# Batch 0's linear term from (h w1) w_out, its hwd in four pieces, and pooling sums two units at a time

## The chip, the cores and the metric

The kernel runs on one core of one Trainium2 chip. The metric is device time in microseconds (us). A core has five engines with instruction queues of their own: TensorE (PE in the profile, with its weight loads as PEld), VectorE (DVE), ScalarE (ACT), GpSimd (POOL) and SyncE (SP), and 16 DMA engines. TensorE writes its results to PSUM, which has 8 banks of 128 partitions by 512 fp32 values; VectorE and ScalarE carry them on to SBUF.

## What is computed

```python
# x (4, 12544, 128), inducing (32, 128); w1, w2 (128, 1024); w_out (1024, 128)
def mab(q, kv):
    s = scale * (q @ kv.transpose(0, 2, 1))     # scale = 1 / sqrt(128)
    s = s - s.max(-1, keepdims=True)
    a = np.exp(s)
    a /= a.sum(-1, keepdims=True) + 1e-09
    return a @ kv
h = mab(I, x)              # I: inducing for each of the 4 batches; h is (4, 32, 128)
y = mab(x, h)              # (4, 12544, 128)
t = y.reshape(50176, 128)
out = np.maximum(t @ w1, t @ w2) @ w_out        # (50176, 128)
```

The kernel never builds y. With e the exponentials of a token over the 32 rows of h, and d their sum, t = (e h) / d, and

out = (e (h w1) w_out + relu(e h(w2 - w1)) w_out) / d.

The first term is the linear term: `m1` = (h w1) w_out is 32 x 128 for each batch. `hwd` is h(w2 - w1), 32 x 1024 for each batch. A chunk is 128 tokens; there are 98 chunks in each of 4 batches, 8 final matmuls (one for each 128 of the 1024 hidden values) for each chunk, 3136 in all.

## The kernel before

Everything is recorded in the order in which a small clock in the kernel believes it best. Batch 0 has a first part of its own (transposes, scores, sums). Then the main loop goes through the finals of all batches and puts between them the phases, the stages of exponentials and the pooling of the next batch. The queues of the engines hold what was recorded, in that order.

The handover from batch 0's sums to the loop:

```python
nc.vector.tensor_scalar(out=w1h, in0=w1h, scalar1=-1.0, ...)
sums = small_h(0)          # hT4: h transposed, four copies side by side; es: the sums of exponentials
weights_2()                # transposes of w1h -> w1T
small_sums(*sums)          # rs, rw: reciprocals of the sums, with scales
stage(blocks[0])
small_hwd(0, (0,))
blocks[0].staged = max(blocks[0].staged, st[0]["hwdr"])
small_hwd(0, (1,))
stage(blocks[1])
# ...
phase(plan_phase(False))
weights_3()                # w1out = w1 w_out
phase(plan_phase(False))
pending.append((small_m1, (0,)))
```

```python
def small_hwd(b, halves=(0, 1)):
    # ...
    for half in halves:
        for n in range(2 if b == 0 and half == 0 else 1):
            w = 256 if b == 0 and half == 0 else 512
            # ...
            if b == 0:
                nc.tensor.matmul(out=ps, lhsT=hT4, rhs=w2h[:, sl], start=True, stop=False)
                nc.tensor.matmul(out=ps, lhsT=hT4, rhs=w1h[:, sl], start=False, stop=True)
            else:
                nc.tensor.matmul(out=ps, lhsT=hT4, rhs=w21[:, sl], start=True, stop=True)
            # half 0, n 0: VectorE to hwd (times rw for batch 0); the others: ScalarE
            # ...

def small_m1(b):           # m1 = h w1out
    nc.tensor.matmul(out=ps[:, 0:128], lhsT=hT4, rhs=w1out, start=True, stop=True)
    # ... VectorE to m1bd and m1

def weights_2():           # 2 banks of 4 transposes: one copied by VectorE, one by ScalarE
    # ...
def weights_3():           # 8 matmuls w1T x woutp in one bank, then ScalarE to w1out
    # ...
```

(`hT4`, `ps` stand for the entries of `st[b]` and the bank taken.) One unit of pooling, 16 chunks of the next batch; a batch has six units and two chunks over:

```python
def pool_accum(b, u):
    bi, ps = bank([128, 512])
    # ...
    for j in range(4):
        for g in range(4):
            nc.tensor.matmul(out=ps[32 * g : 32 * (g + 1), 0:128],
                             lhsT=eT[:, j, 32 * g : 32 * (g + 1)],
                             rhs=xn_of(b, U * u + 4 * g + j),
                             start=(j == 0), ..., tile_position=(0, 32 * g))
    # ... last unit: the two chunks over, and their sums
    if u == 0:
        nc.vector.tensor_copy(out=hacc, in_=ps[:, 0:128])
    else:
        nc.vector.tensor_add(out=hacc, in0=ps[:, 0:128], in1=hacc)
```

In the loop, a phase (`phase`, line 957) is up to four row-packed jobs, one for each quarter of 32 partitions, each of 512 columns into a bank of its own: e times hwd for relu, or e times m1 for the linear term. Each bank of relu is evicted by ScalarE (line 973) or VectorE (line 976). A final (`final_one`, line 792) is one 128x128 matmul of relu by woutp. A group of up to 4 chunks, 32 finals, is evicted by VectorE (line 819, times the reciprocal of d) and stored. `stage` (line 582, line 594) makes the exponentials of a block; `dens` (line 622) their sums. `keep_busy` (line 749) puts in matmuls of zeros where the kernel's clock expects TensorE to wait:

```python
for _ in range(n):
    nc.tensor.matmul(out=g.ps[:, 0:256], lhsT=warm[:, 0:128], rhs=warm[:, 0:256],
                     start=False, stop=False, skip_group_check=True)
```

Three forms of TensorE's array alternate: the whole array (finals, sums, transposes), packed by rows (phases), packed by columns (stage, pooling).

The relu buffers have two slots for each quarter; w2h and w1h are loaded into a slot of quarters 0 and 1:

```python
w2h = relup.tile([128, 4096], F16, name="w2h", tag="relu0")[:, 0:J]
w1h = relup.tile([128, 4096], F16, name="w1h", tag="relu1")[:, 0:J]
```

Of the kernel before, what the change touches and what calls it, by code (L numbers as in the profile page):

```python
# [9 lines left out]
F16 = mybir.dt.float16  # L10
F32 = mybir.dt.float32
AF = mybir.ActivationFunctionType
# [90 lines left out]
def kernel(  # L103
# [93 lines left out]
    with tc.manual_schedule(engines={ET.PE, ET.DVE, ET.Activation, ET.Pool, ET.SP}):  # L197
# [150 lines left out]

        def pool_accum(b, u):
            bi, ps = bank([128, 512])  # L350
            ck.wait(ck.bank[bi], "p1")
            eT = st[b]["eT", u][0]
            st[b]["sum", u] = True
            last = u == NU - 1
            for j in range(4):
                for g in range(4):
                    nc.tensor.matmul(  # L357
                        out=ps[32 * g : 32 * (g + 1), 0:128],
                        lhsT=eT[:, j, 32 * g : 32 * (g + 1)],
                        rhs=xn_of(b, U * u + 4 * g + j),  # L360
                        start=(j == 0),
                        stop=(j == 3 and not (last and g < REST)),
                        tile_position=(0, 32 * g),
                        skip_group_check=True,
                    )
            if last:
                et = st[b]["et"][0]
                for g in range(REST):
                    for rhs, lo, n in ((xn_of(b, U * NU + g), 0, 128), (ones16[:, 0:1], 128, 1)):
# [8 lines left out]
                        )  # L378
            end = ck.run(0.26, "col")
            if u == 0:  # L380
                st[b]["hacc"] = smp.tile([128, C], F32, name=f"hacc_{b}", tag="hacc")
                nc.vector.tensor_copy(out=st[b]["hacc"], in_=ps[:, 0:128])
            else:
                acc = st[b]["hacc"]
                nc.vector.tensor_add(out=acc, in0=ps[:, 0:128], in1=acc)
# [61 lines left out]

        def small_hwd(b, halves=(0, 1)):
            if 0 in halves:
                st[b]["hwd"] = smp.tile([128, J], F16, name=f"hwd_{b}", tag="hwd")  # L450
            hwd = st[b]["hwd"]
            for half in halves:
                for n in range(2 if b == 0 and half == 0 else 1):
                    w = 256 if b == 0 and half == 0 else 512
                    bi, ps = bank([128, 512])
                    ps = ps[:, 0:w]
                    sl = slice(512 * half + w * n, 512 * half + w * (n + 1))
                    ck.wait(max(ck.bank[bi], st[b]["hT4r"]), "p1")
                    if b == 0:
                        nc.tensor.matmul(out=ps, lhsT=st[b]["hT4"], rhs=w2h[:, sl], start=True, stop=False)  # L460
                        nc.tensor.matmul(out=ps, lhsT=st[b]["hT4"], rhs=w1h[:, sl], start=False, stop=True)
                        end = ck.run(0.43 * w / 512)
                    else:
                        nc.tensor.matmul(out=ps, lhsT=st[b]["hT4"], rhs=w21[:, sl], start=True, stop=True)  # L464
                        end = ck.run(0.215)
                    if half == 0 and n == 0:
                        if b == 0:
                            nc.vector.tensor_scalar(
                                out=hwd[:, sl], in0=ps, scalar1=st[0]["rw"], scalar2=None, op0=ALU.mult
                            )  # L470
                        else:
                            nc.vector.tensor_copy(out=hwd[:, sl], in_=ps)
                        ck.bank[bi] = ck.on_dve(end, 0.07 + w / 970.0)
                    else:
                        nc.scalar.activation(
                            out=hwd[:, sl], in_=ps, func=AF.Copy, scale=st[0]["rw"] if b == 0 else 1.0
                        )
                        ck.bank[bi] = ck.on_act(end, 0.06 + w / 1200.0)
                    st[b]["hwdr"] = max(ck.bank[bi], st[b].get("hwdr", 0.0))

        def small_m1(b):
            bi, ps = bank([128, 512])
            ck.wait(max(ck.bank[bi], st[b]["hT4r"]), "p1")
            nc.tensor.matmul(out=ps[:, 0:128], lhsT=st[b]["hT4"], rhs=w1out, start=True, stop=True)
            end = ck.run(0.06)
            m1 = smp.tile([128, C], F16, name=f"m1_{b}", tag="m1")
            bd = {0: [0], B - 1: [0, 1, 2, 3]}.get(b, [])
            outs = [(m1bd[32 * q : 32 * (q + 1), q, :], slice(32 * q, 32 * (q + 1))) for q in bd]
            for o, r in outs + [(m1, slice(0, 128))]:
                if b == 0:  # L490
                    nc.vector.tensor_scalar(
                        out=o, in0=ps[r, 0:128], scalar1=st[0]["rw"][r, :], scalar2=None, op0=ALU.mult
                    )
                else:
                    nc.vector.tensor_copy(out=o, in_=ps[r, 0:128])
                ck.bank[bi] = ck.on_dve(end, 0.2)
            st[b]["m1"] = m1
            st[b]["m1r"] = ck.bank[bi]
# [15 lines left out]

        def weights_2():
            for g in range(2):
                bi, ps = bank([128, 4, 128], F16)
                ck.wait(ck.bank[bi], "w")
                for j in range(4):
                    jb = 4 * g + j  # L520
                    nc.tensor.transpose(ps[:, j, :], w1h[:, 128 * jb : 128 * (jb + 1)], identity16)
                end = ck.run(0.056 * 4)
                if g == 0:
                    nc.vector.tensor_copy(out=w1T[:, 0:4, :], in_=ps)
                    ck.bank[bi] = ck.on_dve(end, 0.4)
                else:
                    nc.scalar.copy(out=w1T[:, 4:8, :], in_=ps)
                    ck.bank[bi] = w_of["w1T"] = ck.on_act(end, 0.5)

        def weights_3():  # L530
            bi, ps = bank([128, 512])
            ck.wait(max(ck.bank[bi], w_of["w1T"]), "w")
            for jb in range(NJB):
                nc.tensor.matmul(
                    out=ps[:, 0:128],
                    lhsT=w1T[:, jb, :],
                    rhs=woutp[:, jb, :],
                    start=(jb == 0),
                    stop=(jb == NJB - 1),
                )  # L540
            end = ck.run(0.056 * NJB)
            nc.scalar.mul(out=w1out, in_=ps[:, 0:128], mul=-1.0)
            ck.bank[bi] = w_of["w1out"] = ck.on_act(end, 0.2)
# [24 lines left out]
        def stage(blk):  # L568
# [29 lines left out]
            blk.staged = ck.bank[bi] = ck.on_act(end, 0.05 + wd * 128 / 1200.0)  # L598
            blk.staged = max([blk.staged] + [st[qu.b].get("hwdr", 0.0) for qu in some])
        relu_of = {}  # L600
# [88 lines left out]
        sums = small_h(0)  # L689
        weights_2()  # L690
        small_sums(*sums)
        stage(blocks[0])
        small_hwd(0, (0,))
        blocks[0].staged = max(blocks[0].staged, st[0]["hwdr"])
        small_hwd(0, (1,))
        stage(blocks[1])


# [200 lines left out]
        def phase(jobs):  # L899
# [6 lines left out]
            for (kind, q, a, u), bi in zip(jobs, free):  # L906
                _, ps = bank([128, 512], only=bi)
                ready = max(ck.bank[bi], a.blk.staged if kind == "L" else a.staged)
                if kind == "L":
                    ready = max(ready, st[a.blk.b]["m1r"])  # L910
# [48 lines left out]
            for kind, q, a, u, bi, ps, _ in got:  # L959
# [11 lines left out]
                ready = end + 0.03  # L971
                if max(ck.act, ready) + 0.477 <= max(ck.dve, ready) + 0.597:
                    nc.scalar.activation(out=dst, in_=src, func=AF.Relu)  # L973
                    t = ck.on_act(ready, 0.477)
                else:
                    nc.vector.tensor_scalar(out=dst, in0=src, scalar1=0.0, scalar2=None, op0=ALU.max)  # L976
                    t = ck.on_dve(ready, 0.597)
                ck.bank[bi] = t
# [12 lines left out]
        for b in range(1, B):  # L991
            base = DONE0[b - 1]
            t_first, t_step = (6, 2.2) if b == 1 else (-6, 3.4)
            for u in range(NU):
# [6 lines left out]
                at(base + int(turn), pool_turn, b, u)  # L1001
                at(base + int(acc), pool_accum, b, u)
            s, end = int(s), base + int(acc)
# [10 lines left out]
        def ready(f, a):  # L1014
# [17 lines left out]
            if f is small_h:  # L1032
                return d.get("haccr", INF) <= now
            if f in (small_hwd, small_m1):
                if f is small_m1 and a[0] == 0 and w_of["w1out"] > now:
                    return False
                return d.get("hT4r", INF) <= now
            return True

        COL = (pool_scores, pool_accum)  # L1040
        FULL = (pool_rest, small_rep, small_h, small_hwd, small_m1)

# [33 lines left out]
        def want_stage(ahead):  # L1076
# [11 lines left out]
            )  # L1088

        phase(plan_phase(False))  # L1090
        weights_3()
        phase(plan_phase(False))
        pending.append((small_m1, (0,)))
        state["stage"] = 2
        weights_1b()
# [65 lines left out]
```

The softmax here doesn't subtract the row's maximum and nothing guards it: scores larger than these inputs give would overflow.

## Time and profile before

| what | value |
|---|---|
| device time, median of 3 runs | 330.14 us (329.71 to 330.32) |
| span of the profiled execution | 328.5 us |
| granted TensorE clock | 1.00 |
| DMA moved | 53.65 MB, 163 GB/s mean |
| finals (line 792) | 3136, 218.1 us busy |
| relu evictions on ScalarE (line 973) / VectorE (line 976) | 463 of 604 ns / 321 of 681 ns |
| fillers (line 749) | 13 |
| pooled sums: matmuls (line 357) / evictions to hacc (lines 382 and 385) | 288 / 18 |

The page gives for each engine the busy time, its share of the span and the number of instructions; a group of instructions reads as line, engine, operation, output<-input, shapes and count, then busy time and mean ns of one, then the idle time before them. Mean durations include the time in which a pipelined instruction overlaps its neighbours, so pace is better read from starts.

### The profile page before, as it was taken

What the parts mean: (1) busy time and instruction counts of PE and PEld (TensorE: products, weight loads), DVE (VectorE), ACT (ScalarE), POOL (GpSimd) and SP (SyncE); (2) the same over time, 40 slices, a digit from 0 to 9 for tenths busy, and PEclk for the clock granted to TensorE, in tenths of its full rate; (3) what the DMA queues carried; (4) which work ended last, traced back from release to release, by engine and by line L of the source; (5) the groups of instructions that cost most, each with busy time, mean ns of one, the idle gap of its engine ahead of it and who ended that gap; (6) DMA issues with size and microseconds to landing.
All of it is one profiled execution on the core that took longest, in us unless ns stands there. A gap on an engine that the chain in (4) does not pass through costs nothing.

```text
span 328.5 us, 12601 instructions
## 1 busy us (share of the span) xinstructions
PE 322.6 (98%) x5401; PEld 244.1 (74%) x5401; DVE 285.3 (87%) x532; ACT 280.7 (85%) x562; POOL 25.7 (8%) x54
## 2 busy tenths in 40 slices
PE   8999999999999999999999999999999999999996
PEld 3876777777777777777777777777777777778785
DVE  3359899999988999998989989988989989989873
ACT  3679899998789999988888999998968999999961
POOL 7351030000310000000040000000000000000000
PEclk9999999999999999999999999999999999999999
DMA  8999999964299999672479999983212312222233
GB/s 207 208 206 213 289 237 205 216 187 124 57 227 244 229 221 213 167 155 97 132 139 245 226 257 215 197 177 100 98 66 97 114 67 99 98 98 98 80 116 114
DMA packets 70823, 53.65 MB, mean 163 GB/s; under 512 B 52176, under 2 KB 55408, under 8 KB 70768
## 3 DMA queue, kind: packets, MB, share of 16 engines
q1 hardware_dynamic: 64656, 38.63, 47.4%
q0 software_dynamic: 6112, 14.22, 22.1%
q8 instruction: 42, 0.69, 0.9%
q14 instruction: 13, 0.11, 0.1%
HBM read 28.33 MB, written 25.69 MB: 164 GB/s over the span
## 4 chain that ended last, share of the span: by engine, by line
PE 96%; DVE 1%; issue 1%; ACT 0%; DVEq 0%; ACTq 0%
PE ps L792 60%; PE ps L957 22%; PE ps L582 3%; PE ps L232 2%; PE ps L357 1%; PE ps L309 1%; PE ps L648 1%; PE ps L248 1%; PE ps L280 1%; PE ps L622 1%; DVE relu L976 1%; PE ps L749 1%; PE ps L271 1%; PE ps L640 0%; PE ps L464 0%
## 5 line engine op out<-in xcount | busy, mean ns | idle before, releaser
L973 ACT ACTIVATE relu<-ps 128x512 f16<-128x512 f32 x463 | 244.6, 604 | 31.1 <-PE ps L957 24.1
L976 DVE TENSOR_SCALAR relu<-ps 128x512 f16<-128x512 f32 x321 | 205.8, 681 | 18.8 <-PE ps L957 17.9
L792 PE MATMUL ps<-woutp,relu 128*128 128x128 f16 x3136 | 218.1, 220 | 0.0
L792 PEld LDWEIGHTS <-relu 128*128 128x128 f16 x3136 | 177.3, 98 | 39.4 <-issue 28.3
L957 PE MATMUL ps<-e,hwd 32*128 32x512 f16 (+2 forms) x880 | 89.0, 360 | 0.0
L819 DVE TENSOR_TENSOR o<-ps,rp 128x512 f32<-128x512 f32 (+3 forms) x108 | 68.6, 635 | 5.7 <-PE ps L792 3.1
L957 PEld LDWEIGHTS <-hwd 32*128 32x128 f16 x880 | 25.0, 91 | 21.1 <-issue 0.8
L957 PE MATMUL ps<-m,e 32*128 32x128 f16 x381 | 38.8, 217 | 0.0
L957 PEld LDWEIGHTS <-e 32*128 32x128 f16 x381 | 21.4, 92 | 2.6
L165 POOL DMA_DIRECT2D xn<-in_x_dram x31 | 16.7, 551 | 8.4 <-DMA xn<-in_x_dram 4.4
L236 DVE COPY xT<-ps 128x512 f16<-128x512 f16 (+3 forms) x11 | 5.5, 504 | 8.1 <-PE ps L232 8.0
L594 ACT ACTIVATE e<-ps 128x512 f16<-128x512 f32 (+2 forms) x21 | 11.6, 572 | 0.0
L320 ACT ACTIVATE eu<-ps 128x512 f16<-128x512 f32 x18 | 10.8, 619 | 0.0
L582 PE MATMUL ps<-xT,hT 128*32 128x512 f16 (+3 forms) x114 | 10.4, 366 | 0.0
L164 POOL COPY pace<-esr 128x1 f32<-128x1 f32 x2 | 0.4, 183 | 116.6 <-DVE esr L391 116.6
L239 ACT COPY xT<-ps 128x768 f16<-128x768 f16 (+3 forms) x11 | 6.1, 557 | 3.0 <-PE ps L232 2.9
L232 PE MATMUL ps<-identity,xn 128*128 128x128 f16 x98 | 7.7, 224 | 0.1
L582 PEld LDWEIGHTS <-hT 128*32 128x32 f16 x114 | 2.9, 93 | 5.9 <-issue 5.2
L232 PEld LDWEIGHTS <-xn 128*128 128x128 f16 x98 | 5.9, 100 | 1.3 <-DVE xn L644 0.9
L257 ACT ACTIVATE et<-ps 128x448 f16<-128x448 f32 (+4 forms) x11 | 4.5, 413 | 2.6 <-PE ps L248 2.6
L632 DVE RECIPROCAL rp<-ps 128x16 f32<-128x16 f32 (+2 forms) x28 | 6.7, 239 | 0.0
L622 PE MATMUL ps<-ones_q,e 128*128 128x4 f16 x102 | 6.5, 165 | 0.0
(96 smaller groups left out, 117.5 us busy)
## 6 DMA issues: line engine op xcount, KB each, us to landing
out_dram<-o SPq DMA_DIRECT2D x90, 256.0 KB, 2.5
xn<-in_x_dram POOLq DMA_DIRECT2D x24, 448.0 KB, 11.9
out_dram<-o SPq DMA_DIRECT2D x10, 128.0 KB, 3.1
xn<-in_moe_w_dram POOLq DMA_DIRECT2D x4, 256.0 KB, 14.1
xn<-in_x_dram POOLq DMA_DIRECT2D x4, 224.0 KB, 10.2
xT<-xn SPq DMA_TRANSPOSE x42, 3.8
xf<-in_x_dram SPq DMA_DIRECT2D x1, 512.0 KB, 3.7
xf<-in_x_dram SPq DMA_DIRECT2D x1, 384.0 KB, 4.1
```

Of the source, the lines that this page charges most:

```text
L165: nc.gpsimd.dma_start(out=xn_at[b, i][:, 0:n, :], in_=xr[b, :, k0 : k0 + n, :])
L232: nc.tensor.transpose(ps[:, j, :], xn[:, g + j, :], identity16)
L320: nc.scalar.activation(out=eu, in_=ps, func=AF.Exp, scale=scale, accum_out=st[b]["es"][:, u : u + 1])
L582: nc.tensor.matmul(out=ps[32 * q : 32 * (q + 1), 128 * t : 128 * (t + n)], lhsT=hq, rhs=xT[:, c : c + n, :], start=True, stop=True, tile_p ...
L594: nc.scalar.activation(out=blk.e2[:, 0 : 128 * wd], in_=ps[:, 0 : 128 * wd], func=AF.Exp, scale=st[0]["rs"] if blk.b == 0 else scale,)
L622: nc.tensor.matmul(out=ps[:, 4 * t : 4 * t + 4], lhsT=blk.e2[:, 128 * t : 128 * (t + 1)], rhs=ones_q, start=True, stop=True,)
L632: nc.vector.reciprocal(out=blk.rp[:, 0:wd, :].rearrange("p t q -> p (t q)"), in_=ps[:, 0 : 4 * wd])
L792: nc.tensor.matmul(out=g.ps[:, 128 * c : 128 * (c + 1)], lhsT=g.blk.relu[q][:, 128 * (jb * w4 + t) : 128 * (jb * w4 + t + 1)], rhs=woutp[: ...
L819: nc.vector.tensor_mul(osb[:, 0:n, :], g.ps[:, 0 : n * C].rearrange("p (s c) -> p s c", s=n), rp)
L957: nc.tensor.matmul(**seq[i])
L973: nc.scalar.activation(out=dst, in_=src, func=AF.Relu)
L976: nc.vector.tensor_scalar(out=dst, in0=src, scalar1=0.0, scalar2=None, op0=ALU.max)
```

## The change

Three things. For batch 0, the linear term no longer goes through w1out = w1 w_out: h w1 is made directly (8 matmuls that give it transposed, 32 columns each), and m1 is (h w1) w_out with 32 column-packed matmuls. So w1's transposes and w1out, which batches 1 to 3 still need, leave the head and become jobs of the loop, due from chunks 16 and 18 on. Batch 0's hwd is made in four pieces of 256, evicted by VectorE and ScalarE in turn, and a phase waits only for the pieces that it reads; the stage of block 1 comes after the first phase. And the pooling sums of batches 1 to 3 take two units at a time into one bank, with one eviction. It is meant to let the loop begin with less ahead of it, and to take work from VectorE. Two constants of the kernel's clock (cost of a relu eviction) change as well, so the recorded order of the loop shifts throughout.

```diff
         def pool_accum(b, u):
...
-            for j in range(4):
-                for g in range(4):
-                    nc.tensor.matmul(
...
+            for v in (u - 1, u):
+                eT = st[b]["eT", v][0]
+                st[b]["sum", v] = True
+                for j in range(4):
+                    for g in range(4):
+                        nc.tensor.matmul(
...
+                            start=(j == 0 and v < u),
+                            stop=(j == 3 and v == u and not (last and g < REST)),
...
-            if u == 0:
+            if u == 1:
...
-        def small_hwd(b, halves=(0, 1)):
+        def small_hwd(b, pieces=None):
+            w = 256 if b == 0 else 512
...
+            for n in range(J // w) if pieces is None else pieces:
...
+                if n % 2 == 0:
+                    # VectorE to hwd[:, sl]
+                else:
+                    # ScalarE to hwd[:, sl]
+                for jb in range(w * n // 128, w * (n + 1) // 128):
+                    st[b]["hwdr", jb] = ck.bank[bi]
+        def small_hw1():
+            for jb in range(NJB):
+                nc.tensor.matmul(out=ps[:, M * jb : M * (jb + 1)], lhsT=w1h[:, 128 * jb : 128 * (jb + 1)],
+                                 rhs=st[0]["hT4"][:, 0:M], start=True, stop=True)
+            nc.scalar.mul(out=hw1T.rearrange("p j m -> p (j m)"), in_=ps[:, 0 : NJB * M], mul=-1.0)
+        def small_m1_0(_=0):
+            for jb in range(NJB):
+                for q in range(4):
+                    nc.tensor.matmul(out=ps[32 * q : 32 * (q + 1), 0:128], lhsT=st[0]["hw1T"][:, jb, :],
+                                     rhs=woutp[:, jb, :], start=(jb == 0), stop=(jb == NJB - 1),
+                                     tile_position=(0, 32 * q), skip_group_check=True)
+            # VectorE, times rw, to m1bd and m1
...
-        def weights_2():
-            for g in range(2):                 # 4 transposes and a copy each
+        def weights_2(_=0):                    # 8 transposes in one bank, one copy by VectorE
...
         sums = small_h(0)
-        weights_2()
         small_sums(*sums)
         stage(blocks[0])
-        small_hwd(0, (0,))
-        blocks[0].staged = max(blocks[0].staged, st[0]["hwdr"])
-        small_hwd(0, (1,))
-        stage(blocks[1])
+        small_hwd(0, (0, 1))
...
-                if max(ck.act, ready) + 0.477 <= max(ck.dve, ready) + 0.597:
+                if max(ck.act, ready) + 0.487 <= max(ck.dve, ready) + 0.608:
...
-                at(base + int(acc), pool_accum, b, u)
+                if u % 2:
+                    at(base + int(acc), pool_accum, b, u)
...
+        small_hwd(0, (2, 3))
         phase(plan_phase(False))
-        weights_3()
+        stage(blocks[1])
+        state["stage"] = 2
+        small_hw1()
         phase(plan_phase(False))
-        pending.append((small_m1, (0,)))
-        state["stage"] = 2
+        pending.append((small_m1_0, (0,)))
+        at(16, weights_2, 0)
+        at(18, weights_3, 0)
```

(Cut; comments stand for lines of the same content.)

## The prediction

> **What bounds the kernel now.** I read the page's busy shares and its chain first, then the windows by stage, then the timeline of the handover from batch 0's sums to the main loop.
>
> ```profile
> PE 322.6 (98%) x5401; PEld 244.1 (74%) x5401; DVE 285.3 (87%) x532; ACT 280.7 (85%) x562; POOL 25.7 (8%) x54
> ...
> PE 96%; DVE 1%; issue 1%; ACT 0%; DVEq 0%; ACTq 0%
> ```
>
> TensorE (PE) has work in hand for 98% of the span, and the chain that ended last runs 96% through it. "Busy" includes the drain of a pipelined matmul, so I also take the pace of the loop from the chain in order of time (start, duration, what):
>
> ```profile
> 39.82 0.89 PE ps L792 x14
> 41.03 0.89 PE ps L792 x14
> 42.25 0.89 PE ps L792 x14
> ...
> 177.95 0.83 PE ps L792 x13
> 179.11 0.83 PE ps L792 x13
> 180.27 0.83 PE ps L792 x13
> ```
>
> A round of 14 final matmuls and one phase takes 1.215 us, one of 13 takes 1.16. So a final costs 0.055 and the trip to a phase and back 1.16 - 13 x 0.0555 = 0.43. Rounds repeat to the hundredth over the whole loop: TensorE waits for nobody there, and whatever is added to its queue is paid. The windows say so too (PE and DVE busy in 50 us):
>
> ```profile
> 100.00:150.00 50.00, 50.00 (x831) 37.50 (x827) 47.54 (x84) 45.98 (x93) 0.00 (x0) 1.00 0.96 200
> ```
>
> VectorE at 47.5 of 50 is close behind. The start of the loop is another regime (timeline, start, duration):
>
> ```profile
> 27.68 0.72 PE L749 MATMUL ps<-warm 128*128 128x256 f16 x5
> 28.33 0.40 PE L957 MATMUL ps<-e,hwd 32*128 32x512 f16 x6
> 28.66 0.72 PE L749 MATMUL ps<-warm 128*128 128x256 f16 x5
> ...
> 27.70 5.50 ACT L973 ACTIVATE relu<-ps 128x512 f16<-128x512 f32 x10 [0.23 <-PE ps L957]
> ...
> 27.84 3.06 DVE L976 TENSOR_SCALAR relu<-ps 128x512 f16<-128x512 f32 x5
> ```
>
> Line 749 is the filler of keep_busy. From about 24.8 to 31 us ScalarE (0.55 per relu) and VectorE (0.61) evict without a gap and TensorE fills time: the evictions are the bound there, not TensorE.
>
> **What the Trainium skill says.** "TensorEngine Tiling (Array Packing)", Key Properties: "Changing tiling mode (not just tile) drains the TensorE". The trace agrees in kind: a phase's four packed 512-column rows need about 0.22 and the trip takes 0.43, so two changes cost some 0.1 each. "TensorE: Matmul & The Clock Gate", Back-to-back issue gap, gives about 81 ns for 128-column matmuls in a stream with weight loads; the trace has 55.5, which I use. "ScalarE: Activation LUTs", What ACT_TABLE_LOAD costs: a per-partition pointer operand adds some 93 ns to an ACTIVATE. The trace: hwd with rw 687 ns, without 605, so 82. So each eviction carries a fixed part, and four 256-wide pieces of batch 0's hwd (467 on ScalarE, 485 on VectorE) cost more engine time in all than two of 512, but run side by side.
>
> **The change, part by part.**
>
> *Pooled sums in pairs.* The same 288 matmuls; nine evictions into hacc instead of eighteen.
>
> ```profile
> L385 DVE TENSOR_TENSOR hacc<-ps,hacc 128x128 f32<-128x128 f32 x15 | 4.3, 287 | 0.8
> ...
> L382 DVE COPY hacc<-ps 128x128 f32<-128x128 f32 x3 | 0.8, 281 | 0.0
> ```
>
> That is 9 x 0.287 = 2.6 us off VectorE. On TensorE it could save changes of mode, but in the queue of before most units already stood in twos and threes (32, 48 or 16+16 around other column work). One unit alone costs 0.34 (161.64 to 161.98), two 0.56 (75.12 to 75.68), so joining two separate ones would save 0.11:
>
> ```profile
> 75.12 0.63 PE L357 MATMUL ps<-xn,eT 128*32 128x128 f16 x32
> 75.68 0.51 PE L792 MATMUL ps<-woutp,relu 128*128 128x128 f16 x6
> ...
> 161.64 0.41 PE L357 MATMUL ps<-xn,eT 128*32 128x128 f16 x16
> 161.98 0.62 PE L792 MATMUL ps<-woutp,relu 128*128 128x128 f16 x8
> ```
>
> I counted the changes of mode in both built queues from the end of batch 0's sums: 485 in each. No gain for TensorE.
>
> *Head, hwd.* Before: 4 x 0.11 + 2 x 0.22 = 0.87 (23.01 to 23.98 with the change of mode). After: 8 x 0.11 = 0.88. Same for TensorE. VectorE takes one more piece (0.48, in 0.89 of idle time before its first relu at 24.81), ScalarE 0.467 instead of 0.687.
>
> *Head, linear term.* Leaves: 8 transposes of w1h (21.71 to 22.16, 0.45), their two copies (VectorE 0.42, ScalarE 0.59), 8 matmuls of w1out (0.45), one m1 matmul (0.07). Enters: 8 matmuls of 32 columns (others of that form, line 280, stand 0.025 apart: 0.20), one 256-wide eviction on ScalarE (about 0.4, as hwd's), 32 packed matmuls (a pooled unit's stand 0.0128 apart: 0.41). For TensorE up to the 50th final: -0.45 - 0.45 - 0.07 + 0.20 + 0.41 = -0.36, and by summing the whole two queues, which also place a stage or a phase differently, about -0.5. But evictions bound this stretch. There I get: the sum's matmul no longer waits behind the transposes, some 0.12; stage of block 1 moves behind the first phase, so that comes 0.33 earlier; VectorE's first relu starts about 0.4 earlier; ScalarE's gains 0.2 and loses 0.1 to hw1T against w1out. Averaged over two evicting engines: 0.25 to 0.3 earlier. Fillers up to there: 13 before, 13 after. **-0.3.**
>
> *What moved.* The transposes and w1out are not gone: they stand at final 144 and 162 now, where TensorE is the bound: 0.45 + 0.45. The copy of w1T is one 128x1024 on VectorE (about 0.69, as xT's copies of that shape). **+0.9.**
>
> *What the new order adds.* The built queue of after has 21 fillers, and the 8 more stand near the turns of batches (2, 2 and 1 after finals 1292, 1460 and 1500, and 3 after 2268). Each is 0.11 (110 to 112 apart in the trace): **+0.9**, certain to be issued, though one may cover a wait that before had unfilled. Around a filler some 0.1 stays open, four places: **+0.3**. hwd of batch 1 stands at final 653 instead of 629, of batch 3 at 2229 instead of 2204.
>
> *VectorE's relief.* Net of w1T's and hwd's growth some 1.9 us of 285. Over the loop the rounds hardly wait for it, so I give it **-0.2**.
>
> Sum: -0.3 + 0.9 + 0.9 + 0.3 - 0.2 = +1.6, so 330.14 + 1.6 = 331.7 us.
>
> **The rivals.** (1) *The head gives its whole TensorE saving and the fillers only take the place of old waits.* For it: laying the durations above along the queue of before leaves about 4 us of small waits after the head, some at the turns (0.39 at 239.7, where the rep matmul waits for esr). Then -0.5 + 0.9 + 0.2 gives about 330.5. (2) *VectorE is the hidden bound of the loop* (47.5 of 50), and its 1.9 us come back at perhaps two thirds: 330.4 less the head, about 329.8. Against it: the rounds are equal to the hundredth, which an engine waiting for evictions would not show. (3) *A buffer takes the place of the wait.* w1h lives in a relu slot of quarter 1 and is now read until final 144, so blocks 0, 1 and 2 of that quarter share one buffer: block 1's first write (after final 20) must follow final 24, block 2's (after 139) final 144. VectorE stands in order behind these. I count 4 and 5 finals, 0.2 to 0.3 us each, mostly the time an eviction takes to start anyway. If it lets the eviction-bound head slip: 333. (4) *The next batch starves.* hwd later by 24 finals in two batches means fewer phases in hand and longer true waits than the fillers cover: 333 to 335.
>
> **Range and chances.** The sure part is +0.9 moved and +0.9 fillers; the head could be -0.8 to +0.5, the turns -1 to +2. 8 in 10: 329.7 to 334.0. A 2% step is 6.6 us, more than any term or plausible sum: faster 0.01, within 0.97, slower 0.02.
>
> **What would show it.** Right: first phase near 24.0 instead of 24.31; fillers of the head still there; w1T and w1out inside a stretch of full rounds that are not shortened for it; hacc's group 6 + 3; 21 fillers; 50th final some 0.3 earlier, end of batch 0's finals about 0.5 later, end 1.6 later. Wrong: rounds of 14 below 1.2 us, or idle PE at the turns over 1 us, or a head that differs by over a microsecond.

## The result and the profile after

| | before | after |
|---|---|---|
| device time, median | 330.23 us (329.71 to 330.80) | 333.69 us (332.97 to 333.96) |
| ratio, 95% interval | | 1.0101 (1.0087 to 1.0116) |
| span of the profiled execution | 328.5 us | 330.9 us |
| relu evictions on ScalarE / VectorE | 463 / 321 | 458 / 326 |
| fillers | 13 | 21 |
| idle TensorE from 150 to 260 us, from the windows | 0.40 us | 0.69 us |

The prediction was +1.6 us to 331.7; measured is +3.46. The sign and the range held, the size did not. The two profiled executions are only 2.4 us apart (332.97 against 330.56), because the profile of after was taken in its fastest execution; the other five took 333.64 to 333.96. So about 1 us of the +3.46 stands in neither trace.

Busy shares and chain of the page of after:

```profile
PE 324.0 (98%) x5450; PEld 245.0 (74%) x5450; DVE 286.9 (87%) x529; ACT 278.3 (84%) x557; POOL 25.7 (8%) x54
...
PE 94%; DVE 2%; DMA 1%; ACT 1%; issue 0%; DVEq 0%; ACTq 0%
```

TensorE still bounds the kernel. It is busy for 1.4 us more than before, and its part of the chain went from 96% to 94%. VectorE, which the pairs were to relieve, is busier than before (286.9 against 285.3), though its groups for hacc (by form) shrank as they should, to 6 + 3:

```profile
L387 DVE TENSOR_TENSOR hacc<-ps,hacc 128x128 f32<-128x128 f32 x6 | 1.7, 284 | 0.2 <-PE ps L372 0.2
...
L384 DVE COPY hacc<-ps 128x128 f32<-128x128 f32 x3 | 0.9, 284 | 0.1
```

Five relu evictions (681 ns each) came to VectorE and the copy of w1T (680 ns) too. The head by the timeline of TensorE in after (start, duration):

```profile
23.39 0.53 PE L987 MATMUL ps<-e,hwd 32*128 32x128 f16 x9
```

The first phase starts at 23.39 instead of 24.31; the eight matmuls of hw1 follow at 24.18, and the 32 packed ones at 26.00. The moved work, in the chain in order of time of after (start, duration, what):

```profile
42.36 0.45 PE ps L557 x8
...
42.86 0.33 PE ps L987 x3
43.19 0.01 issue
43.20 0.37 PE ps L987
...
45.40 0.45 PE ps L566 x8
```

The transposes and w1out take 0.45 each; the rounds around them keep their pace (14 finals in 0.89). The phase at 42.86 takes 0.71 instead of 0.33, for its last job waits until 43.20. By the trace it waits for VectorE's relu eviction of 42.46 to 43.15, which had itself begun 0.39 late (timeline of VectorE):

```profile
42.46 0.69 DVE L1006 TENSOR_SCALAR relu<-ps 128x512 f16<-128x512 f32 x1 [0.39 <-ACT relu L1003]
43.06 0.68 DVE L846 TENSOR_TENSOR o<-ps,rp 128x512 f32<-128x512 f32 x1
43.66 0.68 DVE L559 COPY w1T<-ps 128x1024 f16<-128x1024 f16 x1
```

An output and the copy of w1T follow it, so they are not what the phase waits for. Why the eviction began late was not found: the ScalarE relu that the trace names had ended at 42.19, and with the head alone (head_warm, below) VectorE has no such gap there.

To see where the time came from I took the starts of the finals in the traces of several kernels, counted from the last matmul of batch 0's sums, and the time between some of them (us). A row of this table can also change because work stands on the other side of its border; the last line can not. The first entry of before is high for its head: the other kernels with the old head in this table have 4.21 to 4.23.

| finals | before | pairs_only | head_warm | consts_only | pairs_consts | after |
|---|---|---|---|---|---|---|
| sums to 1 | 4.47 | 4.23 | 3.85 | 4.21 | 4.21 | 3.76 |
| 1 to 50 | 7.73 | 7.73 | 8.23 | 7.73 | 7.73 | 8.23 |
| 50 to 144 | 8.54 | 8.54 | 8.72 | 8.54 | 8.54 | 8.72 |
| 144 to 200 | 5.24 | 5.24 | 7.12 | 5.20 | 5.20 | 6.90 |
| 200 to 784 (end of batch 0) | 58.73 | 57.42 | 57.75 | 59.01 | 58.26 | 56.96 |
| 784 to 1300 | 49.16 | 50.19 | 49.16 | 48.91 | 49.12 | 49.13 |
| 1300 to 1568 (end of batch 1) | 26.38 | 26.57 | 26.39 | 28.38 | 28.45 | 28.45 |
| 1568 to 2352 (end of batch 2) | 75.55 | 75.14 | 75.57 | 76.45 | 76.12 | 76.12 |
| 2352 to 3136 | 67.49 | 67.06 | 67.49 | 68.00 | 67.70 | 67.70 |
| sums to 3136 | 303.28 | 302.11 | 304.30 | 306.43 | 305.34 | 305.99 |

The kernels of the inner columns come from the experiments: the pairs alone, the head alone (with eight matmuls of zeros, which keep its clock up, below), the two constants alone, and pairs with constants. Two columns with the same recorded order agree to 0.02 us in a stretch: after and pairs_consts from final 784 on, head_warm and before likewise. So the time of these stretches goes with the recorded order, and is repeated by it. After's +2.7 in the last line is +1.7 in the stretch with w1T and w1out, -1.8 in the one behind it, and +2.9 from final 1300 on, all of which pairs_consts has as well.

What "wait" means below: the time from batch 0's sums to the last final, less what each instruction takes where nothing holds it (final 0.0557, phase's row of four 0.217, filler 0.109, change of mode 0.104). By this sum after has 298.5 us of work, fillers included, and 7.5 of waits, before 297.1 and 6.3: +0.9 for 8 fillers, +0.6 for hw1 and the 32 packed matmuls, -0.1 for m1's own, +1.3 of waits. The fillers stand in waits too, as an experiment below shows, so the waits of after are 2.2 us longer in all.

### The profile page after: what moved, and what is told of

It reads as the page before. It is cut to its first block, busy times and chain, and to the rows that moved or that the text cites. A ratio compares the mean times of both kernels' runs of the same rounds, so it can differ in the third digit from the quotient of the medians.

```text
span 330.9 us, 12686 instructions
## 1 busy us (share of the span) xinstructions
PE 324.0 (98%) x5450; PEld 245.0 (74%) x5450; DVE 286.9 (87%) x529; ACT 278.3 (84%) x557; POOL 25.7 (8%) x54
## 4 chain that ended last, share of the span: by engine, by line
PE 94%; DVE 2%; DMA 1%; ACT 1%; issue 0%; DVEq 0%; ACTq 0%
PE ps L819 59%; PE ps L987 22%; PE ps L614 2%; PE ps L232 2%; DVE relu L1006 2%; PE ps L359 1%; PE ps L309 1%; DMA xf<-in_x_dram 1%; PE ps L248 1%; PE ps L653 1%; PE ps L280 1%; ACT relu L1003 1%; PE ps L271 1%; PE ps L671 0%; PE ps L776 0%
## 5 line engine op out<-in xcount | busy, mean ns | idle before, releaser
L1006 DVE TENSOR_SCALAR relu<-ps 128x512 f16<-128x512 f32 x326 | 209.9, 681 | 21.6 <-PE ps L987 18.9
```

## The experiments

The expectations weigh theories against each other: K, the two constants cost the time; T, the pairs do; H, the head with the work that it moves does; S, any new order moves the time by a microsecond or two. G (the clock) and L (the lead) come later.

**The three parts apart.** Each is the changed kernel or the one before with part of the diff. head_only leaves the pairs and the constants out:

```diff
 after -> head_only
-                if u % 2:
-                    at(base + int(acc), pool_accum, b, u)
+                at(base + int(acc), pool_accum, b, u)     # pool_accum as before
-                if max(ck.act, ready) + 0.487 <= max(ck.dve, ready) + 0.608:
+                if max(ck.act, ready) + 0.477 <= max(ck.dve, ready) + 0.597:
```

> The head's part alone: the kernel after with single pooled units and the old two constants of the clock (0.477, 0.597). Its queue has 12 fillers, none after the head. Theory K (the constants of the clock, not the head or the pairs, cost the time: they put in late fillers and reorder the turns): within 0.7 us of before, 329.6 to 330.9. Theory T (the pairs cost it, by a later hwd at the turns): the same. Theory H (moving w1's transposes, w1out and a whole w1T copy into the full rounds costs it): +1.5 to +3, that is 331.7 to 333.2.

Measured: 331.66 us, 1.0041 (1.0022 to 1.0060), at the lower edge of theory H. Its ten times lie in two groups. In four of them (332.4 to 332.7) the mean granted clock of the execution was 0.993 to 0.995; in the other six (331.1 to 331.3, and one of 332.0) it was 0.999 or more, and their median is 331.27. More on this clock below.

```diff
 before -> pairs_only
-                at(base + int(acc), pool_accum, b, u)
+                if u % 2:
+                    at(base + int(acc), pool_accum, b, u)    # pool_accum as after
```

> The pooling pairs alone on the kernel before, old constants: 13 fillers, none late; hwd of batch 1 at final 673 instead of 629. Theory K: within 0.7 us of before. Theory T: +1.5 to +3 (331.7 to 333.2), with waits at the turns of batches. Theory H: within 0.7 us. If VectorE was a hidden bound: 1 us or more faster.

Measured: 329.38 us, 0.9974 (0.9964 to 0.9983): faster than before, and the fastest kernel of this study. Of the readings put on record, that of a hidden bound on VectorE (1 us or more faster) comes nearest. VectorE is busy for 281.8 us by its page. Two of its windows (behind the span the busy time of PE, PEld, DVE, ACT and POOL, then clock, DMA share and GB/s):

```profile
150.00:200.00 50.00, 50.00 (x856) 38.07 (x844) 45.61 (x85) 46.24 (x92) 4.00 (x9) 1.00 0.85 185
200.00:260.00 60.00, 59.97 (x1035) 45.38 (x1034) 54.10 (x103) 53.88 (x110) 0.00 (x0) 1.00 0.55 130
```

The same windows of before, then those of after with one more, which the prediction shows of before:

```profile
150.00:200.00 50.00, 49.92 (x849) 38.17 (x847) 45.43 (x87) 44.62 (x88) 4.00 (x9) 1.00 0.82 189
200.00:260.00 60.00, 59.68 (x1029) 45.19 (x1030) 55.65 (x107) 52.63 (x108) 0.00 (x0) 1.00 0.53 129
```

```profile
100.00:150.00 50.00, 50.00 (x830) 37.89 (x828) 45.20 (x79) 44.36 (x91) 0.00 (x0) 1.00 1.02 211
150.00:200.00 50.00, 49.78 (x824) 36.88 (x822) 46.39 (x87) 44.10 (x88) 4.00 (x9) 1.00 0.86 186
200.00:260.00 60.00, 59.53 (x1026) 45.18 (x1025) 56.01 (x104) 51.79 (x106) 0.00 (x0) 1.00 0.49 125
```

From 150 to 260 us TensorE is idle for 0.03 us in pairs_only, 0.40 in before and 0.69 in after. From 200 us on VectorE has 54.1 of 60 us in pairs_only against 56.0 in after, with ScalarE the other way round.

```diff
 before -> consts_only
-                if max(ck.act, ready) + 0.477 <= max(ck.dve, ready) + 0.597:
+                if max(ck.act, ready) + 0.487 <= max(ck.dve, ready) + 0.608:
-                    t = ck.on_act(ready, 0.477)
+                    t = ck.on_act(ready, 0.487)
-                    t = ck.on_dve(ready, 0.597)
+                    t = ck.on_dve(ready, 0.608)
```

> The two constants alone (0.487, 0.608) on the kernel before: 21 fillers in the queue, 8 of them late (after finals 668, 1500, 2268), as many as in the kernel after. Theory K: +1.5 to +3 (331.7 to 333.2): 0.9 of fillers and as much of waits at the turns. Theories T and H: within 0.7 us. Theory S (every reordering moves the time by a microsecond or two, whatever it was for): anything between -1.5 and +3, and then head_only and pairs_only scatter just as much.

Measured: 333.81 us, 1.0105 (1.0090 to 1.0120). Two numbers in the kernel's clock, no work added but what it then records itself, cost the kernel before as much as the whole change does. It has 8 late fillers too, waits of 8.2 us against 6.3, and ten relu evictions more on VectorE (331 to ScalarE's 453). So 8 late fillers, which the prediction charged to the new order, come with the constants alone. What the constants do once head and pairs are in is another matter, below.

**Do the fillers cost?** after_nofill has after's queue without its 8 late fillers (a filler adds zeros to a bank of finals, so what is computed stays).

```diff
 after -> after_nofill
-            for _ in range(n):
+            for _ in range(n if state["done"] < 100 else 0):
```

> The kernel after in the very same order, but the 8 fillers after the head left out. If they displace work: 0.7 to 0.9 us faster than after, some 332.9. If they cover waits that are there anyway (in the trace of after two of the four places still wait 0.17 and 0.22 behind their fillers, two don't): 0 to 0.4 faster, 333.3 to 333.7.

Measured: 334.15 us, 1.0113 (1.0098 to 1.0129), no gain; nor is there one in its two executions with the clock up, 333.87 and 333.88. The place of the first late filler by the timeline of TensorE, in after and then in after_nofill:

```profile
153.43 0.34 PE L819 MATMUL ps<-woutp,relu 128*128 128x128 f16 x3
153.61 0.38 PE L776 MATMUL ps<-warm 128*128 128x256 f16 x2
153.99 0.40 PE L819 MATMUL ps<-woutp,relu 128*128 128x128 f16 x4
```

```profile
154.87 0.34 PE L819 MATMUL ps<-woutp,relu 128*128 128x128 f16 x3
155.44 0.40 PE L819 MATMUL ps<-woutp,relu 128*128 128x128 f16 x4 [0.22 <-ACT relu L1003]
```

From the first to the second group of finals it is 0.56 us with two fillers and 0.57 without: the next final waits for a relu of ScalarE in either case. From final 50 to the last the two traces take 293.99 and 293.98 us. The fillers stand wholly in waits, and the 0.9 that they showed as busy is wait by another name. The profile of after_nofill does begin its loop 1.1 us later (final 50 at 13.13 after the sums, not 12.00); that led to the clock.

**The clock in the head.** Windows of 1 us of head_only, then one of after; the granted clock is the third column from the end (0.50 in the two windows left out as well):

```profile
21.00:22.00 1.00, 0.78 (x12) 0.58 (x11) 0.44 (x2) 0.39 (x2) 0.53 (x1) 0.97 1.82 208
22.00:23.00 1.00, 1.00 (x8) 0.47 (x8) 0.32 (x2) 0.23 (x1) 0.53 (x1) 0.50 1.17 210
...
25.00:26.00 1.00, 1.00 (x24) 0.60 (x21) 0.87 (x2) 0.86 (x3) 0.00 (x0) 0.83 1.08 221
```

```profile
22.00:23.00 1.00, 1.00 (x12) 0.70 (x12) 0.48 (x3) 0.47 (x1) 0.36 (x1) 1.00 1.17 208
```

In the profiles of head_only, after_nofill and after_oldconst the clock falls to half for 0.06 + 3 + 0.34 = some 3.4 us at the very start of the loop, and the first final comes at 4.8 to 5.1 us behind the sums instead of 3.76. After's profile kept 1.00 in all these windows. The mean granted clock, on record for every execution, tells how often this happens: 3.4 us at half in some 332 lower it to 0.995 (an estimate from these two numbers). It was 0.993 to 0.995 in 4 of 10 executions of head_only, 3 of 5 of after_nofill and 3 of 4 of after_oldconst, but 0.999 or more in all six of after. So the drop has no part in the +3.46. The Trainium skill, "TensorE: Matmul & The Clock Gate", Part 1, says that the array goes to half its clock after at least one idle window of about 3.4 us, and back after a busy one. Half and 3.4 us agree with the trace. The idle window does not: by the trace's count TensorE is busy for 0.78 of the us before and for more in those ahead of it. What the head lost is the transposes, matmuls of 128 columns that stood just there. That this loss is the cause is a conjecture, and one kernel may speak against it: before_c450 (below), which has the transposes, shows 0.993 to 0.994 in three of its six executions; no trace tells at what place. The next two put eight 128x128 matmuls of zeros in that place, with no other instruction moved:

```diff
 after -> after_warm, head_only -> head_warm
+        wb, wps = bank([128, 512])
+        for _ in range(8):
+            nc.tensor.matmul(out=wps[:, 0:128], lhsT=warm[:, 0:128], rhs=warm[:, 0:128],
+                             start=True, stop=True)
         small_sums(*sums)
```

> The kernel after, with eight 128x128 matmuls of zeros into a free bank where the kernel before had the transposes of w1h; everything else in the same order. In head_only and after_nofill the granted TensorE clock is 0.50 from about 22 to 25.5 us, and the first final comes 1.3 us later than in the one profile of after where it stayed 1.00. Theory G (the idle gaps left by the transposes drop the clock in most executions): clock 1.00 throughout, 0.8 to 1.2 us faster than after, 332.5 to 332.9. Rival (evictions bound the head anyway, so the clock there costs nothing): 333.5 to 334.1.

Measured: 333.08 us (332.75 to 333.88), 1.0089 (1.0073 to 1.0106).

> head_only with eight 128x128 matmuls of zeros where w1h's transposes stood; same order. Theory G (head_only's cost is the clock at 0.50 from 22 to 25.4 us): clock 1.00, first final 1.3 us earlier, 330.2 to 330.7. Rival (w1's transposes, w1out and the long copy in the full rounds cost it): 331.2 to 331.7.

Measured: 331.65 us (331.49 to 332.02), 1.0043 (1.0031 to 1.0055). Both profiles show the clock at 1.00 and the first final at 3.85. after_warm fell between theory G and its rival, head_warm on the rival's side. In 25 executions of five kernels with the zeros the mean clock was never below 0.998, in 25 of the new head without them it fell in 10; so the zeros do keep the clock up. A drop costs 1.1 us of start by the traces; to the end it costs head_only 1.4 us (medians of the two groups), but only 0.4 in after_nofill. Since after had no drop at all, the 0.6 by which after_warm is faster (the intervals overlap) is not the clock's.

**Are the parts additive?**

```diff
 after -> after_oldconst (head and pairs)      before -> pairs_consts (pairs and constants)
-   0.487 / 0.608                              -   at(..., pool_accum, b, u)       0.477 / 0.597
+   0.477 / 0.597                              +   if u % 2: at(..., pool_accum, b, u)   0.487 / 0.608
```

> The kernel after with the two constants of before (0.477, 0.597): head and pairs without the third part. If the parts add (head +1.35, pairs -0.93): 330.7, between 330.3 and 331.3. If it was the pairs together with the head that lost at the turns, and not the constants: 332.5 or more.

Measured: 333.61 us, 1.0103 (1.0088 to 1.0118), no faster than after, where head and pairs apart sum to 330.7. By what was put on record this speaks for a loss of pairs and head together, and not for the constants: once these two are in, the constants cost nothing more (333.61 without them, 333.69 with them).

> The kernel before with the pairs and the new constants, without the new head. Its late fillers stand where those of after stand. If the parts add: 333.8 - 0.9 = 332.9, between 332.4 and 333.4. If the constants' cost was an accident of one order (theory S): 329.5 to 332.

Measured: 332.40 us, 1.0066 (1.0054 to 1.0079). Going from before to after in this order, the steps are: constants +3.5 (333.81), pairs -1.4 (332.40), head +1.3 (333.69). In another order they are others: head +1.35 (331.66), pairs +1.95 (333.61), constants +0.1. Head and constants without the pairs were not run.

So after_oldconst needs a reason of its own for being slow. In its timeline of TensorE batch 2's pool scores wait at the turn from batch 1, 1.24 us in all:

```profile
121.36 0.38 PE L309 MATMUL ps<-xT,inducingT 128*32 128x512 f16 x1 [0.50 <-DMA xT<-xn]
```

hwd of batch 1 stands at final 689 there (629 before, 653 in after), and batch 2's transposes of x come late (issued from 106.72 on). Four fillers stand after final 716. Two kernels tell this wait from the clock, both with the zeros in the head, one with constants that bring hwd to final 673:

```diff
 after_warm -> hp_warm            after_warm -> hp_warm_c472
-   0.487 / 0.608                 -   0.487 / 0.608
+   0.477 / 0.597                 +   0.472 / 0.590
```

> The changed kernel with the constants of before (.477/.597) and eight 128x128 matmuls of zeros in its head, so head and pairs without constants and without the drop of the clock. hwd of batch 1 still at final 689. If the clock's drop cost after_oldconst (333.6) what the trace says, 0.6 to 1.3 us: 332.3 to 333.0, with the wait of 1.24 us for the transposed x of batch 2 still there. If the drop costs the median nothing (as between head_only and head_warm): 333.6.

Measured: 333.36 us, 1.0085 (1.0068 to 1.0102). The clock, up again (0.998), gives back little. The wait is there again, in the timeline of TensorE:

```profile
119.63 0.38 PE L309 MATMUL ps<-xT,inducingT 128*32 128x512 f16 x1
120.17 0.39 PE L309 MATMUL ps<-xT,inducingT 128*32 128x512 f16 x2 [0.16 <-DMA xT<-xn]
121.08 0.38 PE L309 MATMUL ps<-xT,inducingT 128*32 128x512 f16 x1 [0.52 <-DMA xT<-xn]
```

From the first of the four scores to the instruction behind them (121.38) it is 1.75 us, where four without a wait take 0.33 (the chain of after at 149.58).

> The same with .472/.590, where hwd of batch 1 stands at final 673 as in pairs alone, so batch 2's loads start earlier. If that wait is what makes head and pairs not additive: no wait over 0.5 us at the turn to batch 2, and 331.65 (head with zeros) less 0.9 (pairs) plus 0.4 to 0.7 (.472 against .477) = 331.2 to 331.5. If head and pairs together cost more for another reason: 332.3 or more.

Measured: 331.69 us, 1.0043 (1.0030 to 1.0056). As expected the wait is gone, but not for the reason put on record. The transposes are issued at 115.24 and 117.61, hardly earlier than in hp_warm (115.81 and 118.17). The scores stand later in the order, in one group of eight:

```profile
125.33 0.68 PE L309 MATMUL ps<-xT,inducingT 128*32 128x512 f16 x8
```

The time is 0.2 above the range given for it. With the wait 1.7 us are gone, and by the traces 1.6 of them between finals 784 and 1300, where the wait stood (52.24 against 50.65): in hp_warm the kernel's clock had put the scores ahead of their data. This is the changed kernel with two other constants and a warm head, and it is 2.0 us faster than after. It is still 1.6 slower than the pairs with the same constants and the old head (pairs_c472, 330.12); by the traces 1.05, all of it ahead of final 784 (84.69 against 83.64).

**The constants as a dial.** They act only through the order. Do they act by themselves, or does any other order scatter as much? The edit of consts_only with other values, on the kernel before, on pairs_only and on after_warm:

```diff
-   0.477 / 0.597
+   0.450 / 0.5625, 0.460 / 0.575, 0.472 / 0.590, 0.482 / 0.602, 0.500 / 0.625
```

> The kernel before with the two constants raised further (0.500, 0.625): 44 fillers, 31 of them late. Theory K, a slower believed eviction costs in proportion: 31 x 0.11 = 3.4 of fillers and some 2 of waits, 335 to 337. Theory S: no order in it, 329 to 334.

> The kernel before with the two constants lowered (0.450, 0.5625), nothing else. Lead, the finals' worth of phases that TensorE has issued ahead (4 for each evicted unit, less the finals done, mean over finals 60 to 3000 of the built queue): 78.2 at 0.500 (335.0 us), 84.3 at 0.487 (333.8), 101.4 at 0.477 (330.3), and 110.9 here. Theory L (time follows the lead, about 0.2 us for each final): 328.3 if straight, 328.5 to 329.8 as the waits run out. Rival (a clock that believes in faster evictions than the chip makes sends TensorE into waits): 330.5 or more.

> The kernel before with pairs and the constants at 0.460, 0.575: lead 108.7, no late filler. Theory L: 1 us under pairs_only's 329.4, 328.0 to 329.0. Rival: 329.4 or more.

> The whole change with eight matmuls of zeros in the head and the constants at 0.460, 0.575: lead 110.1, no late filler, hwd of batch 1 at final 639. If theories G and L are the whole story, the change is then no slower than before: 328.0 to 329.2, some 5 us faster than after. If something else in the change costs time: 330 or more.

> The kernel before with the two constants at .472/.590 (lead of the phases a little above before's; 12 fillers, none late; hwd of batches 1 to 3 at finals 652, 1441, 2214). Theory L (time follows the constants smoothly with an optimum near .477): between 330.3 and 331.5. Theory S (every re-ordering moves the time by 1 to 2 us, constants as such mean nothing): anything from 329 to 334.

> The kernel before with .482/.602, half way to the change's .487/.608 (15 fillers, 2 of them late, at final 2268). Theory L: half way between 330.3 and 333.8, so 331.5 to 332.5. Theory S: anything from 329 to 334.

> The kernel before with the sums in pairs and .472/.590 (12 fillers, none late; hwd at 673, 1410, 2204). Theory L: between pairs with .460 (330.6) and pairs with .477 (329.4), so 329.4 to 330.2. Theory S: 329 to 333.

> The kernel before with the sums in pairs and .482/.602 (13 fillers, none late; hwd at 609, 1420, 2203; 481 changes of mode, the fewest). Theory L: half way between pairs with .477 (329.4) and with .487 (332.4), so 330.4 to 331.4. Theory S: 329 to 333. Were late fillers the sign of the loss rather than the constant: 329.4 or less.

Measured (median us; the lead is how far, in finals, relu jobs recorded are ahead of the finals done, averaged over the recorded queue):

| ScalarE's constant | before's other parts | lead | with pairs | lead | head (with zeros) and pairs | lead |
|---|---|---|---|---|---|---|
| .450 | 333.97 (1.0088 to 1.0134) | 111 | | | | |
| .460 | | | 330.62 (1.0000 to 1.0018) | 109 | 332.06 (1.0039 to 1.0064) | 110 |
| .472 | 330.73 (0.9994 to 1.0017) | 100 | 330.12 (0.9979 to 0.9995) | 104 | 331.69 (1.0030 to 1.0056) | 106 |
| .477 | 330.3 | 101 | 329.38 (0.9964 to 0.9983) | 102 | 333.36 (1.0068 to 1.0102) | 102 |
| .482 | 331.49 (1.0025 to 1.0043) | 94 | 330.44 (0.9984 to 1.0006) | 102 | | |
| .487 | 333.81 (1.0090 to 1.0120) | 84 | 332.40 (1.0054 to 1.0079) | 85 | 333.08 (1.0073 to 1.0106) | 86 |
| .500 | 335.04 (1.0129 to 1.0157) | 78 | | | | |

The third pair of columns is hp_warm_c460, hp_warm_c472, hp_warm and after_warm. Of the times, .450 is a mixture: three executions with the clock up took 332.9 to 333.2, three with it down 334.8 to 335.0.

The first two columns are lowest at .477 and rise to both sides (from .477 to .472 in the first by 0.4, within the interval). The third is not: with the new head .477, where hp_warm shows its wait for the transposed x, is the slowest and .472 the fastest. So the constants have no cost of their own that holds for every kernel; what they cost is what the order that they make costs. Theory L, that time follows the lead, missed where the lead is largest (.450, .460, and .460 with the new head, all expected below 330), and .482 with pairs has an unchanged lead and loses 1.06 us. It fits only the right slope: a believed dearer eviction makes the clock record phases later, and there is less in hand when a batch turns. The four runs at .472 and .482 came within 0.1 us of the ranges that L had given by then, which were drawn between measured neighbours, but inside those of theory S as well, and the third column shows how far one order can stand out. Whether the first two are smooth curves or the scatter of different orders is not shown by so few points. What makes the other orders slower was not found.

## Why the prediction was right and wrong

*What bounds the kernel:* right in the main. TensorE kept 98%, and rounds their 0.89 and 0.33. "TensorE waits for nobody there" was too strong: before has 6.3 us of waits behind batch 0's sums, and 0.40 us of idle time in the windows from 150 to 260 us, which the prediction does not show. (The trip to a phase is 0.44 by its own numbers, not 0.43; nothing hangs on it.)

*Head, -0.3:* the start was better than said, the balance near. The first phase came at 23.39 (said: 24.0) and the first final 0.7 earlier behind the sums, but by final 50 only 0.19 was left (12.00 against 12.19). Even that is the slow start of before's one profile: pairs_only, consts_only and pairs_consts, with the old head, have their 50th final at 11.94 to 11.96. So the new head gained nothing there. The fillers stayed. That the evictions took the gain back, as the prediction had it, fits this but was not tested alone.

*What moved, +0.9:* the two pieces of 0.45 are there, in rounds that are not shortened. In after one phase beside them waits 0.39, which had not been counted. The head alone, with its clock up, makes the last final 1.0 later (304.30 against 303.28), all of it before final 784, against the +0.6 of the two steps. Over the whole kernel its TensorE work rises by the 0.6 of hw1 and the packed matmuls less 0.06, for nothing that left the head was saved, only moved.

*What the new order adds, +0.9 and +0.3:* **this step failed.** It took the 8 late fillers as work "certain to be issued", at its price, and the waits around them as a rest of 0.3. In the trace after has 2.2 us more of waits than before: 0.9 that the fillers fill and 1.3 that nothing fills. The fillers are the mark of waits, not their cause: without them the time is the same. The loss comes late: from final 1300 on after takes 2.9 us longer than before, part of it work put off from batch 0, with an order and a time that pairs_consts has as well, so the new head is not needed for it. pairs_consts differs from pairs_only by the two constants alone, which the prediction does not price at all (they are only named in the account of the change): +3.0 us, by the sum of work and waits 0.9 in filled and 2.35 in unfilled waits. On the kernel before they cost +3.5. But they are one way to such waits and not the only one: with the old constants head and pairs together come out as slow (after_oldconst, 333.61), with the largest of their waits elsewhere, between finals 784 and 1300. So what the prediction missed is the waits that a new order makes. Why this order waits where another does not stays open. Rival 4 was nearest: hwd of the next batch late, true waits longer than the fillers cover, 333 to 335. The longer waits are there, but late hwd is not shown as their cause: pairs_only has hwd of batch 1 later still (final 673) and is faster than before.

*VectorE's relief, -0.2:* with the old head too small: there the pairs give -0.9 at the old constants, -0.6 at .472, -1.05 at .482 and -1.4 at .487. With the new head and the old constants they cost 1.7 to 1.95 instead (head_warm to hp_warm, head_only to after_oldconst). "The rounds hardly wait for it" was read from stretches in the middle of a batch; waits behind the sums fall from 6.3 to 5.2 us in pairs_only. Whether it is VectorE's 3.5 us less of busy time or the order that follows was not separated. That the pairs would leave TensorE's own work as it is was right: 297.1 us in before, 297.0 in pairs_only.

*Rivals:* 1 was wrong, since the head saves nothing whole (its sum gives 330.7, not 330.5). 2 had something: the pairs count for 0.9 with the old head. 3 is not settled: finals 50 and 144, behind the two places, are level with before (12.00 and 20.71 against 12.19 and 20.73), but the stretch between them is 0.18 longer with the new head, and one of VectorE's evictions begins 0.39 late just behind final 144.

*The signs:* 21 fillers and 6 + 3 came as said. The end of batch 0's finals did not: level (84.58 against 84.69) instead of 0.5 later, since the new order puts off part of batch 1's work. It is paid from final 1300 to 1568: 0.9 for two phases more, 0.4 for a pooled pair, 0.3 for fillers and 0.5 for waits.

## What to carry over

In a kernel that is recorded by a clock of its own, a constant of that clock is a change like any other: price it before the parts that look like work. Here the change brought it nearer to the pace of the chip (0.54 to 0.55 on ScalarE, 0.61 on VectorE, against .477 and .597 before and .487 and .608 after) and cost the kernel before 3.5 us, so a truer number is not a better one. With the new head and the pairs in place the same step cost nothing, and pairs that had gained 0.9 lost 1.7: parts of such a change do not add, so try each on both kernels. Fillers tell where an engine waits; taking them out saves nothing (293.98 against 293.99 us).

## What was unexpected on the chip

- The granted clock fell to 0.50 for some 3.4 us at a place where TensorE was busy for 0.78 of the us before, with small matmuls, and this in 10 of 25 executions of the kernels with the new head. With eight 128x128 matmuls of zeros in that place it fell in none of 25.
- A recorded order repeats itself closely: in different kernels, with different heads, the 2352 finals behind batch 0, recorded in one and the same order, took 219.22 us in pairs_c472 (302.86 - 83.64) and 219.24 in hp_warm_c472 (303.93 - 84.69).
- At the turn to batch 2 one instruction of SyncE that issues a DMA transpose of x took 6.46 us (at 108.83 in after_oldconst; 6.47 in hp_warm and 6.14 in hp_warm_c472), while its neighbours took 1.2 to 2.0; the next one was issued only at 116.01. Other kernels have it shorter at that place (3.45 in after, 5.67 in pairs_only). Why was not tried.
